# Down projection with W_down as the moving operand and one store, and the last 64 rows of W_gate and W_up on partitions 0 to 63

## The chip, the cores and the metric

The kernel runs on one core of one Trainium2 chip. The metric is the device time of one execution in microseconds (us); lower is better. Times of several executions are given as a median. The profile describes one further execution, taken by the hardware profiler.

## The reference

One step of a decoder block for four sequences (B = 4), one new token each, all data in bf16. D is 576, F is 4608. The attention has 32 query heads and 16 key heads of 128 elements and looks at the last 4096 of 16384 cached positions.

```python
h  = x + attention(layernorm(x))            # q = ln(x) @ wq; K and V from the caches; @ wo
g  = layernorm(h)
gate = g @ W_gate                           # [4, 576] @ [576, 4608]
up   = g @ W_up
hh   = gate * (gate > 0) * up               # ReGLU
out  = h + hh @ W_down                      # [4, 4608] @ [4608, 576]
```

## The kernel before

All five engines have a program of their own (`prog_sync`, `prog_pool`, `prog_act`, `prog_dve`, `prog_pe`), written out by hand. The class `Sched` gives every operation a name; a dependence on a name becomes a wait on the semaphore of the engine or transfer that makes it. Each engine runs its program in the order written. An operation that waits holds up all that follows on its engine.

**Transfers.** One list, `transfers`, in the order in which SyncE (SP in the profile) issues them: wq, then for each of the 64 pairs of sequence and key head one piece of K and one of V (1 MB each, 128 partitions), wo among them, then W_gate and W_up in four pieces of 128 rows each (`("wg", c)`, `("wu", c)`, 1.15 MB, one row of 9216 bytes per partition), then their last 64 rows (`("wg", 4)`, `("wu", 4)`), then W_down in five pieces (`WD`, of 3, 3, 3, 2 and 1 groups of 384 rows). K, V, wq and the four large pieces of W_gate and W_up use 14 slots of the tile `pool`, and a transfer into a slot waits until its last user is done (lines 188, 191 and 211 of the profile are these issues). W_down (line 223) takes the place of the K slots and waits for the last transposition of K, `("TR", 63)`; so do the last 64 rows (line 217).

The last 64 rows of W_gate and W_up: each row is cut into two halves of 2304 columns, and the 128 halves lie on 128 partitions, row r on partitions 2r and 2r + 1. For this the last 64 elements of the normalized vector are needed twice, once on even partitions and once on odd ones. A matmul with `dup` (`HDUP`) copies them to 128 partitions, and two DVE products with `par` (`HN40`, `HN41`) put zeros on the other half (`hn4`). One matmul with eight moving columns then gives a chunk of each half.

**Attention.** For each pair DVE transposes K into one of three buffers of the tile `kT` (line 344), TensorE forms scores (`qk`), and six pairs later the sum over V (`pv`). The softmax runs on batches of four pairs through DVE, POOL (the maximum over partitions, line 263) and ACT (exp, line 293). After the last pair come the projection with wo and the second layernorm, whose result is `hnT` (five chunks of D on partitions, four columns).

**Gate and up.** The weights are the stationary operand: 128 rows of D by 128 columns of F are loaded, and the four columns of `hnT` move through them. The chunks of F land in one bank of PSUM with F on partitions (`GUB`). ACT takes the relu of the gate (line 299), DVE multiplies with up (line 423); the result `hhT` has F on partitions, 36 chunks of four columns.

**Down.** W_down is the stationary operand too. For each of the 36 chunks of F and each of the five chunks of D (four of 128 columns, one of 64) one matmul with four moving columns adds to PSUM, D on partitions; that is 180 matmuls, five pieces, each piece after its own transfer. DVE adds the residual (`F2`, line 425, `F1`, line 427), transposes 32 x 32 blocks (line 429), and four small transfers store the output, two on SP and two on ACT (`out_part`, line 234). The residual is in `R_sb[:, 0]`, fp32, D on partitions.

All matmuls of `mm` have line 436 in the profile; its weight loads are the rows PEld of the same line.

Of the kernel before, what the change touches and what calls it, by code (L numbers as in the profile page):

```python
# [20 lines left out]
F = 4608  # L21
FC = F // 128
DC = 5
NPAIR = B * KVH
# [6 lines left out]
NKS = 6  # L31
# [7 lines left out]
JJ = 3  # L39
GD = 3  # L40
NG = FC // JJ
HALF = F // 2

ENGS = ("sync", "scalar", "vector", "gpsimd", "tensor")

# [54 lines left out]
def bass_sequential_preLN__sliding_block_cached__glu_gated_reglu__decode_kernel(  # L100
# [12 lines left out]
    with ExitStack() as es:  # L113
        cnt = [0]

        def sb(name, shape, dt):
            return es.enter_context(nc.sbuf_tensor(name, shape, dt))

        pool = sb("pool", [128, NSLOT, SLOT], BF16)
        wo_sb = sb("wo_sb", [128, NWO, SLOT], BF16)  # L120
        kT = sb("kT", [128, NKT, WIN // 2], FP32)
        ident_b = sb("ident_b", [128, 128], BF16)
        ones_f = sb("ones_f", [128, 128], FP32)
        sel = sb("sel", [128, 4, 4, 32], BF16)
        eps_c = sb("eps_c", [128, 1], FP32)
# [8 lines left out]
        dup = sb("dup", [64, 128], BF16)  # L134
        par = sb("par", [128, 2], FP32)
# [15 lines left out]
        hn4 = sb("hn4", [128, 2, B], BF16)  # L151
        gate_sb = sb("gate_sb", [128, FC, B], FP32)
        hhT = sb("hhT", [128, FC, B], BF16)
        h2T = sb("h2T", [128, 32], BF16)
        out_sb = sb("out_sb", [128, 32], BF16)
# [3 lines left out]
        WOB, STB, GUB, DNB, DN4 = 5, 4, 6, 7, 2  # L159
        tpv = pb[TPB][:, :].bitcast(BF16)  # L160

        S = Sched()
# [4 lines left out]
        transfers = []  # L167
# [42 lines left out]
                add((kind, c), "V", None,  # L210
                    lambda e, s, c=c, W=W: e.dma_start(out=pool[:, s, 0:F], in_=W[c * 128:(c + 1) * 128, :]))  # L211

        S4 = NKS - 1
        last_tr = [("TR", i) for i in range(NPAIR - NKS, NPAIR)]
        for u, (kind, W) in enumerate((("wg", B_W_gate), ("wu", B_W_up))):
            transfers.append(((kind, 4), f"gu4_{u}", ("TR", NPAIR - 1),
                              lambda e, u=u, W=W: e.dma_start(out=pool[:, S4, u * HALF:(u + 1) * HALF],  # L217
                                                              in_=W[512:576, :].rearrange("r (u n) -> (r u) n", u=2))))
# [8 lines left out]
        def land(name):  # L227
            return ("L",) + (name if isinstance(name, tuple) else (name,))


        def out_part(S, eng, q):
            nc_ = DC if q < 2 else DC - 1
            dst = out.rearrange("b s d -> (b s) d")
            S.dma(eng, lambda e: e.dma_start(
                out=bass.AP(tensor=dst.tensor, offset=dst.offset + 32 * q, ap=[[128, nc_], [D, B], [1, 32]]),
                in_=out_sb[32 * q:32 * q + 4 * nc_, :]), f"out{q}", deps=["OUT"], name=("STORED", q))


        def prog_sync(S):
            for name, key, free, make in transfers:  # L240
                S.dma("sync", make, key, deps=[free], name=land(name))
            for q in (0, 2):
                out_part(S, "sync", q)
            for q in (0, 2):
                S.wait("sync", ("STORED", q))


        def prog_pool(S):
            g = "gpsimd"
            S.op(g, lambda e: e.memset(eps_c[:, :], EPS), name="EPS")  # L250
            S.op(g, lambda e: e.memset(ident_b[:, :], 0.0), name="P0")
            S.op(g, lambda e: e.affine_select(out=ident_b[:, :], in_=ident_b[:, :], pattern=[[-1, 128]],  # L252
                                              compare_op=ALU.not_equal, fill=1.0, base=0, channel_multiplier=1),
                 deps=["P0"], name="IDB")
# [3 lines left out]
            S.op(g, lambda e: e.memset(h2T[:, :], 0.0), name="H20")  # L258
            for n in range(NBATCH):
                deps = [("RMAX", n)]  # L260
                if n >= 2:
                    deps.append(("SUB", n - 2))
                S.op(g, lambda e, n=n: e.partition_all_reduce(bcm[:, n % 2, :], pmax[:, n % 2, :], 128, bass_isa.ReduceOp.max),  # L263
                     deps=deps, name=("PAR", n))


        def prog_act(S):
# [31 lines left out]
            S.op(a, lambda e: e.activation(out=gate_sb[:, :, :], in_=pb[GUB][:, 0:FC * B].rearrange("p (f b) -> p f b", b=B),  # L299
                                           func=ACT.Relu),  # L300
                 deps=[("GU", 4)], name="A_GATE")
            for q in (1, 3):
                out_part(S, a, q)
            for q in (1, 3):
                S.wait(a, ("STORED", q))


        def prog_dve(S):
# [108 lines left out]
            nmr_bc = bass.AP(tensor=st2, offset=32, ap=[[40, 128], [0, DC], [1, B]])  # L417
            S.op(v, lambda e: e.tensor_tensor(out=tmp5[:, :, :], in0=R_sb[:, 0, :, :], in1=rstd_bc, op=ALU.mult), deps=["S7"], name="N1")
            S.op(v, lambda e: e.tensor_tensor(out=hnT[:, :, :], in0=tmp5[:, :, :], in1=nmr_bc, op=ALU.add), deps=["N1"], name="N2")
            for u in range(2):  # L420
                S.op(v, lambda e, u=u: e.tensor_scalar(out=hn4[:, u, :], in0=pb[STB][:, 256:256 + B], scalar1=par[:, u:u + 1], scalar2=None, op0=ALU.mult),
                     deps=["HDUP"], name=f"HN4{u}")
            S.op(v, lambda e: e.tensor_tensor(out=hhT[:, :, :], in0=pb[GUB][:, FC * B:2 * FC * B].rearrange("p (f b) -> p f b", b=B),  # L423
                                              in1=gate_sb[:, :, :], op=ALU.mult), deps=["A_GATE"], name="D_HHT")
            S.op(v, lambda e: e.tensor_tensor(out=h2T[0:64, 16:20], in0=pb[DN4][0:64, 0:B], in1=R_sb[0:64, 0, 4, :], op=ALU.add),  # L425
                 deps=["DOWN4", "H20"], name="F2")
            S.op(v, lambda e: e.tensor_tensor(out=h2T[:, 0:16], in0=pb[DNB][:, 0:16],
                                              in1=R_sb[:, 0, 0:4, :].rearrange("p c b -> p (c b)"), op=ALU.add), deps=["DOWN"], name="F1")
            S.op(v, lambda e: e.transpose(out=out_sb[:, :], in_=h2T[:, :]), deps=["F1", "F2"], name="OUT")


        def prog_pe(S):
            t = "tensor"

            def mm(o, l, r, start, stop, deps=(), name=None, skip=False):
                S.op(t, lambda e: e.matmul(o, lhsT=l, rhs=r, start=start, stop=stop, skip_group_check=skip),  # L436
                     deps=deps, name=name, signal=name is not None)
# [83 lines left out]
                           name="ATTN" if n == DC - 1 and k == H - 1 else None)  # L521
                        first = False
            mm(pb[STB][:, 128:168], ones_f[:, :], R_sb[:, :, :, :], True, True, deps=["D_R"], name="STAT")
            mm(pb[STB][:, 256:256 + B], dup[:, :], hnT[0:64, 4, :], True, True, deps=["N2"], name="HDUP")
            first = True
            gub = pb[GUB][:, 0:2 * FC * B].rearrange("p (u x) -> p u x", u=2)

            def cols(ap, fc):
                g, j = divmod(fc, JJ)
                x0 = g * 128 * JJ + j  # L530
                return ap[:, x0:x0 + 127 * JJ + 1:JJ]
# [6 lines left out]
                           deps=[land((kind, c))] + (["N2"] if first else []) if f == 0 else [], skip=True)  # L538
                        first = False
            for u, kind in ((0, "wg"), (1, "wu")):  # L540
                o = gub[:, u, :].rearrange("p (v x) -> p v x", v=2)
                for f in range(FC // 2):
                    last = u == 1 and f == FC // 2 - 1
                    mm(o[:, :, f * B:(f + 1) * B], cols(pool[:, S4, u * HALF:(u + 1) * HALF], f), hn4[:, :, :], False, last,
                       deps=[land((kind, 4)), "HN41"] if f == 0 else [], name=("GU", 4) if last else None, skip=True)
            first = True
            for k, (g0, g1) in enumerate(WD):
                deps = [land(("wd", k))] + (["D_HHT"] if first else [])
                for n in (4, 0, 1, 2, 3):
                    w = 128 if n < 4 else 64  # L550
                    for g in range(g0, g1):
                        wv = wd_sb[:, g, :].rearrange("p (j n) -> p j n", n=D)
                        for j in range(JJ):
                            last = k == len(WD) - 1 and g == g1 - 1 and j == JJ - 1
                            name = {4: "DOWN4", 3: "DOWN"}.get(n) if last else None
                            o = pb[DNB][:, n * B:(n + 1) * B] if n < 4 else pb[DN4][0:64, 0:B]
                            mm(o, wv[:, j, n * 128:n * 128 + w], hhT[:, g * JJ + j, :], g + j == 0 and n in (0, 4),
                               last and n >= 3, deps=deps, name=name, skip=True)
                            deps = []
# [37 lines left out]
```

## Time and profile before

| what | value |
|---|---|
| median of three runs | 395.9 us (395.9 to 397.0) |
| the profiled execution's own time | 396.46 us |
| its span, first to last instruction | 393.9 us |
| TensorE matmuls, weight loads, busy share | 4946, 4946, 38% and 36% |
| VectorE (DVE), ScalarE (ACT), POOL, busy share | 45%, 19%, 2% |
| read from HBM | 159.58 MB, 405 GB/s over the span |
| W_down's issues on SP, five | 353.8 to 373.9 us, 1.4 to 7.6 us each |
| W_down's first and last matmul group | from 379.74, from 388.09 us |
| the stores' issue | from 390.45 us |

The profiled execution's time holds 2.6 us around its span (launch and end). Times in the profile count from the span's start. In the timeline a row gives start, length, engine, line, operation, result and operands, count, and in brackets the idle time before it with what ended it. In a table by stage a row gives the stage, TensorE's busy time and number of instructions, its granted clock, the mean busy share of the core's 16 DMA engines and what they moved in GB/s. The trace also holds each DMA packet with its start, length and size, and the time of each semaphore increment of a transfer.

### The profile page before, as it was taken

The page shows a single profiled execution, that of the slowest core. Times are in us where ns is not written, and L with a number is a line of the kernel's source. Part 1 is how long each engine was busy: PE and PEld are TensorE (multiplying, and loading weights), DVE is VectorE, ACT ScalarE, POOL GpSimd, SP SyncE. Part 2 cuts the span into 40 slices and gives each one's busy share as a digit, 9 for nine tenths or more (in the row PEclk, how much of TensorE's full clock was granted, in tenths as well). Part 3 has the DMA queues.
Part 4 walks back from the last instruction along what each step waited for, and adds up shares of the span by engine and source line. Part 5 has one row for each costly group of instructions (what it writes and reads, how often), then busy time and mean ns, then how long its engine had stood idle before and what let it go on. Part 6 is the DMA issues. An engine that isn't in the chain of part 4 may idle for free.

```text
span 393.9 us, 10596 instructions
## 1 busy us (share of the span) xinstructions
PE 150.5 (38%) x4946; PEld 143.0 (36%) x4946; DVE 175.6 (45%) x160; ACT 75.3 (19%) x270; POOL 8.6 (2%) x27
## 2 busy tenths in 40 slices
PE   0253532113334333333243333333433333456644
PEld 0253432113334333333233333333433333446643
DVE  0578542245435555555455545453545455302000
ACT  4024030400404040404040404040212121400000
POOL 0200000000000000000000000000000000000000
DMA  8999999999999999999999999999999999999982
GB/s 313 424 418 421 418 414 421 418 416 423 419 417 420 421 418 418 422 419 418 420 422 418 418 420 421 417 421 423 418 419 421 421 419 418 421 423 420 411 361 83
DMA packets 23436, 160.25 MB, mean 407 GB/s; under 512 B 2526, under 2 KB 2530, under 8 KB 5474
## 3 DMA queue, kind: packets, MB, share of 16 engines
q1 hardware_dynamic: 23341, 159.59, 97.8%
q8 instruction: 38, 0.62, 0.6%
q10 hardware_dynamic: 53, 0.01, 0.0%
q14 instruction: 4, 0.03, 0.0%
HBM read 159.58 MB, written 0.00 MB: 405 GB/s over the span
## 4 chain that ended last, share of the span: by engine, by line
DMA 76%; DVE 8%; SPq 7%; PE 4%; issue 3%; ACT 0%; POOL 0%; POOLq 0%
DMA pool<-in_A_k_cache_dram 66%; DVE kT L344 7%; DMA pool<-in_A_v_cache_dram 6%; DMA pool<-in_B_W_down_dram 5%; SPq L223 4%; PE pb L436 4%; SPq L191 1%; SPq L188 1%; DVE sel L318 1%; SPq L205 1%; DVE qblk L382 0%; ACT xn_bf L276 0%; SPq L217 0%; PE pb L443 0%; SPq L211 0%
## 5 line engine op out<-in xcount | busy, mean ns | idle before, releaser
L344 DVE STREAM_TRANSPOSE kT<-pool 128x2048 f32<-128x2048 f32 x64 | 147.5, 2309 | 134.1 <-DMA pool<-in_A_k_cache_dram 134.0
L436 PE MATMUL pb<-qblk,kT 128*128 128x8 bf16 x2048 | 64.9, 169 | 200.6 <-DVE kT L344 197.8
L436 PEld LDWEIGHTS pb<-qblk,kT 128*128 128x128 bf16 x2048 | 59.6, 104 | 206.2 <-DVE kT L344 203.0
L293 ACT ACTIVATE prob<-s_sb 32x64 bf16<-32x64 f32 x256 | 65.9, 257 | 251.3 <-DVE s_sb L360 248.5
L436 PE MATMUL pb<-prob,pool 128*128 128x2 bf16 x2048 | 63.2, 165 | 7.1 <-DMA pool<-in_A_v_cache_dram 4.0
L436 PEld LDWEIGHTS pb<-prob,pool 128*128 128x128 bf16 x2048 | 59.4, 104 | 7.4 <-DMA pool<-in_A_v_cache_dram 4.2
L350 DVE TENSOR_REDUCE pmax<-pb 128x8 f32<-128x256 f32 x16 | 6.8, 424 | 17.8 <-PE pb L436 17.8
L263 POOL PARTITION_ALL_REDUCE bcm<-pmax x16 | 5.9, 367 | 318.6 <-DVE pmax L350 318.6
L436 PE MATMUL pb<-hnT,pool 128*128 128x4 bf16 x288 | 8.3, 166 | 3.1 <-DMA pool<-in_B_W_gate_dram 1.6
L436 PEld LDWEIGHTS pb<-hnT,pool 128*128 128x128 bf16 x288 | 8.0, 104 | 3.4 <-DMA pool<-in_B_W_gate_dram 1.7
L436 PE MATMUL pb<-hhT,pool 128*128 128x4 bf16 (+1 forms) x180 | 7.0, 173 | 5.7 <-DMA pool<-in_B_W_down_dram 5.7
L436 PEld LDWEIGHTS pb<-hhT,pool 128*128 128x128 bf16 (+1 forms) x180 | 6.5, 114 | 6.2 <-DMA pool<-in_B_W_down_dram 6.1
L367 DVE TENSOR_REDUCE rowsum<-prob 128x8 f32<-128x256 bf16 x16 | 6.1, 382 | 4.3 <-ACT prob L293 4.3
L443 PE MATMUL pb<-ident_b,xn_bf 4*128 4x4 bf16 (+1 forms) x5 | 0.4, 174 | 16.7 <-ACT xn_bf L276 16.7
L423 DVE TENSOR_TENSOR hhT<-pb,gate_sb 128x144 bf16<-128x144 f32 x1 | 0.3, 306 | 13.8 <-ACT gate_sb L299 13.8
L360 DVE TENSOR_TENSOR s_sb<-pb,bcm 128x256 f32<-128x256 f32 x16 | 6.2, 387 | 0.5 <-POOL bcm L263 0.5
L443 PEld LDWEIGHTS pb<-ident_b,xn_bf 4*128 4x128 bf16 (+1 forms) x5 | 0.3, 105 | 16.7 <-ACT xn_bf L276 16.7
L436 PE MATMUL pb<-oX,wo_sb 128*128 128x4 bf16 (+1 forms) x160 | 5.5, 172 | 1.3 <-issue 0.9
L436 PEld LDWEIGHTS pb<-oX,wo_sb 128*128 128x128 bf16 (+1 forms) x160 | 5.3, 114 | 1.5 <-issue 0.9
L318 DVE COPY sel<-ident_b 128x128 bf16<-128x128 bf16 x4 | 2.4, 1127 | 7.7 <-POOL ident_b L252 7.7
L425 DVE TENSOR_TENSOR h2T<-pb,R_sb 64x4 bf16<-64x4 f32 x1 | 0.2, 153 | 11.7 <-PE pb L436 11.7
L436 PE MATMUL pb<-xnT,pool 128*128 128x4 bf16 x128 | 3.6, 166 | 0.0
(76 smaller groups left out, 37.6 us busy)
## 6 DMA issues: line engine op xcount, KB each, us to landing
pool<-in_A_k_cache_dram SPq DMA_DIRECT2D x64, 1024.0 KB, 26.9
pool<-in_A_v_cache_dram SPq DMA_DIRECT2D x64, 1024.0 KB, 27.2
wo_sb<-in_A_wo_dram SPq DMA_DIRECT2D x4, 1152.0 KB, 24.7
pool<-in_B_W_gate_dram SPq DMA_DIRECT2D x4, 1152.0 KB, 20.0
pool<-in_B_W_up_dram SPq DMA_DIRECT2D x4, 1152.0 KB, 21.4
pool<-in_A_wq_dram SPq DMA_DIRECT2D x4, 1024.0 KB, 8.5
pool<-in_B_W_down_dram SPq DMA_DIRECT2D x3, 1296.0 KB, 25.9
pool<-in_B_W_down_dram SPq DMA_DIRECT2D x1, 864.0 KB, 17.8
```

Source lines behind the costliest of these rows:

```text
L188: add(("K", i), "K", ("TR", i), lambda e, s: e.dma_start(out=pool[:, s, 0:WIN], in_=kv(A_k_cache, i)))
L191: add(("V", i), "V", ("PV", i), lambda e, s: e.dma_start(out=pool[:, s, 0:WIN], in_=kv(A_v_cache, i)))
L205: lambda e, s, g=g: e.dma_start(out=wo_sb[:, g, :].rearrange("p (q x) -> p q x", q=2), in_=A_wo[g * 1024:(g + 1) * 1024, :].rearrange("(q ...
L223: lambda e, g0=g0, g1=g1: e.dma_start(out=wd_sb[:, g0:g1, :], in_=B_W_down[g0 * 128 * JJ:g1 * 128 * JJ, :].rearrange("(g p j) n -> p g (j ...
L263: S.op(g, lambda e, n=n: e.partition_all_reduce(bcm[:, n % 2, :], pmax[:, n % 2, :], 128, bass_isa.ReduceOp.max), deps=deps, name=("PAR", n))
L293: S.op(a, lambda e, n=n, t4=t4, g=g, sv=sv: e.activation(out=prob[32 * g:32 * g + 32, n % 3, :, 8 * t4:8 * t4 + 8, :], in_=sv[32 * t4:32 * ...
L318: S.op(v, lambda e, ce=ce: e.tensor_copy(out=sel[:, ce, :, :], in_=bass.AP(tensor=ident_b, offset=64 * (ce // 2) + ce % 2, ap=[[128, 128], ...
L344: S.op(v, lambda e: e.transpose(out=dst, in_=src), deps=deps, name=("TR", i))
L350: S.op(v, lambda e: e.tensor_reduce(out=pmax[:, n % 2, :], in_=pb[SC0 + n % 2][:, 0:NB * T * 2].rearrange("p (r t h) -> p r h t", r=NB, h= ...
L360: S.op(v, lambda e: e.tensor_tensor(out=s_sb[:, n % 2, :].rearrange("p (r t h) -> p r t h", r=NB, h=2), in0=pb[SC0 + n % 2][:, 0:NB * T * ...
L367: S.op(v, lambda e: e.tensor_reduce(out=rowsum[:, b, 8 * q:8 * q + 8], in_=prob[:, n % 3, :, :, :].rearrange("p r t h -> p r h t"), axis=A ...
L436: S.op(t, lambda e: e.matmul(o, lhsT=l, rhs=r, start=start, stop=stop, skip_group_check=skip), deps=deps, name=name, signal=name is not None)
```

## The change

Three things are changed, all behind the attention.

1. The last 64 rows of W_gate and W_up go, uncut, to partitions 0 to 63 of the tile `kT`, which the transpositions of K no longer need then. Sixteen transfers of eight rows do this: each takes every fourth partition of a block of 32. They wait for the last scores, `("QK", 63)`. `hn4`, `HDUP` and the two products go; 72 matmuls over 64 rows with four moving columns take the place of 36 over 128 rows with eight.
2. In the down projection `hhT` is the stationary operand (four columns), and W_down moves: two matmuls of 288 columns for each chunk of F, into two banks of PSUM, with the four sequences on partitions 0 to 3. The residual comes into the same sums by six fp32 matmuls of `R_sb` with an identity, `ident_f`, which POOL makes at the start.
3. ACT copies the first 288 columns to `out_sb`, DVE the other 288, and SP stores them with one transfer of four rows.

```diff
-        S4 = NKS - 1
-        last_tr = [("TR", i) for i in range(NPAIR - NKS, NPAIR)]
+        gu4 = kT[:, :, :].rearrange("p n x -> p (n x)").bitcast(BF16)
         for u, (kind, W) in enumerate((("wg", B_W_gate), ("wu", B_W_up))):
-            transfers.append(((kind, 4), f"gu4_{u}", ("TR", NPAIR - 1),
-                              lambda e, u=u, W=W: e.dma_start(out=pool[:, S4, u * HALF:(u + 1) * HALF],
-                                                              in_=W[512:576, :].rearrange("r (u n) -> (r u) n", u=2))))
+            for i in range(8):
+                p0 = 32 * (i // 4) + i % 4
+                transfers.append(((kind, 4) if i == 7 else None, f"gu4_{u}", ("QK", NPAIR - 1),
+                                  lambda e, p0=p0, u=u, W=W: e.dma_start(out=gu4[p0:p0 + 29:4, u * F:(u + 1) * F],
+                                                                         in_=W[512 + p0:512 + p0 + 29:4, :])))
...
-            for q in (0, 2):
-                out_part(S, "sync", q)
-            for q in (0, 2):
-                S.wait("sync", ("STORED", q))
+            S.dma("sync", lambda e: e.dma_start(out=out.rearrange("b s d -> (b s) d"), in_=out_sb[:, :]), "outdma",
+                  deps=["OUT0", "OUT1"], name="STORED")
+            S.wait("sync", "STORED")
...
+            S.op(g, lambda e: e.memset(ident_f[:, :], 0.0), name="P1")
+            S.op(g, lambda e: e.affine_select(out=ident_f[:, :], in_=ident_f[:, :], pattern=[[-1, 128]],
+                                              compare_op=ALU.not_equal, fill=1.0, base=0, channel_multiplier=1),
+                 deps=["P1"], name="IDF")
...
-            for q in (1, 3):
-                out_part(S, a, q)
-            for q in (1, 3):
-                S.wait(a, ("STORED", q))
+            S.op(a, lambda e: e.copy(out=out_sb[:, 0:HD], in_=pb[DNB][0:B, 0:HD]), deps=["DOWN0"], name="OUT0")
...
-            for u in range(2):
-                S.op(v, lambda e, u=u: e.tensor_scalar(out=hn4[:, u, :], in0=pb[STB][:, 256:256 + B], ...),
-                     deps=["HDUP"], name=f"HN4{u}")
...
-            S.op(v, lambda e: e.tensor_tensor(out=h2T[0:64, 16:20], ...), deps=["DOWN4", "H20"], name="F2")
-            S.op(v, lambda e: e.tensor_tensor(out=h2T[:, 0:16], ...), deps=["DOWN"], name="F1")
-            S.op(v, lambda e: e.transpose(out=out_sb[:, :], in_=h2T[:, :]), deps=["F1", "F2"], name="OUT")
+            S.op(v, lambda e: e.tensor_copy(out=out_sb[:, HD:D], in_=pb[DNB + 1][0:B, 0:HD]), deps=["DOWN1"], name="OUT1")
...
-            mm(pb[STB][:, 256:256 + B], dup[:, :], hnT[0:64, 4, :], True, True, deps=["N2"], name="HDUP")
...
-                for f in range(FC // 2):
-                    mm(o[:, :, f * B:(f + 1) * B], cols(pool[:, S4, u * HALF:(u + 1) * HALF], f), hn4[:, :, :], ...)
+                for f in range(FC):
+                    mm(gub[:, u, f * B:(f + 1) * B], cols(gu4[0:64, u * F:(u + 1) * F], f), hnT[0:64, 4, :], ...)
+            for u in range(2):
+                for c in range(DC):
+                    lo, hi = max(c * 128, u * HD), min(c * 128 + 128, D, (u + 1) * HD)
+                    if lo < hi:
+                        w = 128 if c < 4 else 64
+                        mm(pb[DNB + u][0:B, lo - u * HD:hi - u * HD], R_sb[0:w, 0, c, :],
+                           ident_f[0:w, lo - c * 128:hi - c * 128], c * 128 <= u * HD, False, ...)
             for k, (g0, g1) in enumerate(WD):
-                for n in (4, 0, 1, 2, 3):
-                    for g in range(g0, g1):
-                        for j in range(JJ):
-                            mm(o, wv[:, j, n * 128:n * 128 + w], hhT[:, g * JJ + j, :], ...)
+                for f in range(g0 * JJ, g1 * JJ):
+                    g, j = divmod(f, JJ)
+                    for u in range(2):
+                        mm(pb[DNB + u][0:B, 0:HD], hhT[:, f, :],
+                           wd_sb[:, g, j * D + u * HD:j * D + (u + 1) * HD], False, last, ...)
```

More of the change, by code (lines that the diff above doesn't have):

```diff
@@ L42 @@
 HALF = F // 2
+HD = D // 2
 ENGS = ("sync", "scalar", "vector", "gpsimd", "tensor")
@@ L122, in bass_sequential_preLN__sliding_block_cached__glu_gated_reglu__decode_kernel @@
         ident_b = sb("ident_b", [128, 128], BF16)
+        ident_f = sb("ident_f", [128, 128], FP32)
         ones_f = sb("ones_f", [128, 128], FP32)
@@ L150, in bass_sequential_preLN__sliding_block_cached__glu_gated_reglu__decode_kernel @@
         hnT = sb("hnT", [128, DC, B], BF16)
-        hn4 = sb("hn4", [128, 2, B], BF16)
         gate_sb = sb("gate_sb", [128, FC, B], FP32)
         hhT = sb("hhT", [128, FC, B], BF16)
-        h2T = sb("h2T", [128, 32], BF16)
-        out_sb = sb("out_sb", [128, 32], BF16)
+        out_sb = sb("out_sb", [B, D], BF16)
         pb = [es.enter_context(nc.psum_tensor(f"pb{i}", [128, 512], FP32)) for i in range(8)]
         SC0, OB0, SUMB, QB, QR, TPB = 0, 2, 4, 5, 6, 7
-        WOB, STB, GUB, DNB, DN4 = 5, 4, 6, 7, 2
+        WOB, STB, GUB, DNB = 5, 4, 6, 2
         tpv = pb[TPB][:, :].bitcast(BF16)
@@ L228, in land @@
             return ("L",) + (name if isinstance(name, tuple) else (name,))
[L231 to L236, printed above, removed]
         def prog_sync(S):
             for name, key, free, make in transfers:
-                S.dma("sync", make, key, deps=[free], name=land(name))
-            for q in (0, 2):
-                out_part(S, "sync", q)
-            for q in (0, 2):
-                S.wait("sync", ("STORED", q))
+                S.dma("sync", make, key, deps=[free], name=land(name) if name else None)
+            S.dma("sync", lambda e: e.dma_start(out=out.rearrange("b s d -> (b s) d"), in_=out_sb[:, :]), "outdma",
+                  deps=["OUT0", "OUT1"], name="STORED")
+            S.wait("sync", "STORED")
         def prog_pool(S):
@@ L257, in prog_pool @@
             S.op(g, lambda e: e.memset(R_sb[:, :, :, :], 0.0), name="R0")
-            S.op(g, lambda e: e.memset(h2T[:, :], 0.0), name="H20")
+            S.op(g, lambda e: e.memset(ident_f[:, :], 0.0), name="P1")
+            S.op(g, lambda e: e.affine_select(out=ident_f[:, :], in_=ident_f[:, :], pattern=[[-1, 128]],
+                                              compare_op=ALU.not_equal, fill=1.0, base=0, channel_multiplier=1),
+                 deps=["P1"], name="IDF")
             for n in range(NBATCH):
@@ L419, in prog_dve @@
             S.op(v, lambda e: e.tensor_tensor(out=hnT[:, :, :], in0=tmp5[:, :, :], in1=nmr_bc, op=ALU.add), deps=["N1"], name="N2")
-            for u in range(2):
-                S.op(v, lambda e, u=u: e.tensor_scalar(out=hn4[:, u, :], in0=pb[STB][:, 256:256 + B], scalar1=par[:, u:u + 1], scalar2=None, op0=ALU.mult),
-                     deps=["HDUP"], name=f"HN4{u}")
             S.op(v, lambda e: e.tensor_tensor(out=hhT[:, :, :], in0=pb[GUB][:, FC * B:2 * FC * B].rearrange("p (f b) -> p f b", b=B),
                                               in1=gate_sb[:, :, :], op=ALU.mult), deps=["A_GATE"], name="D_HHT")
[L425 to L429, printed above, removed]
+            S.op(v, lambda e: e.tensor_copy(out=out_sb[:, HD:D], in_=pb[DNB + 1][0:B, 0:HD]), deps=["DOWN1"], name="OUT1")
         def prog_pe(S):
@@ L540, in prog_pe @@
             for u, kind in ((0, "wg"), (1, "wu")):
-                o = gub[:, u, :].rearrange("p (v x) -> p v x", v=2)
-                for f in range(FC // 2):
[L543 to L546, printed above, removed]
-            for k, (g0, g1) in enumerate(WD):
-                deps = [land(("wd", k))] + (["D_HHT"] if first else [])
-                for n in (4, 0, 1, 2, 3):
-                    w = 128 if n < 4 else 64
-                    for g in range(g0, g1):
-                        wv = wd_sb[:, g, :].rearrange("p (j n) -> p j n", n=D)
-                        for j in range(JJ):
[L554 to L559, printed above, removed]
@@ new lines, in prog_pe @@
+                for f in range(FC):
+                    last = u == 1 and f == FC - 1
+                    mm(gub[:, u, f * B:(f + 1) * B], cols(gu4[0:64, u * F:(u + 1) * F], f), hnT[0:64, 4, :], False, last,
+                       deps=[land((kind, 4))] if f == 0 else [], name=("GU", 4) if last else None, skip=True)
+            for u in range(2):
[3 more added lines that the diff above has]
+                        w = 128 if c < 4 else 64
+                        mm(pb[DNB + u][0:B, lo - u * HD:hi - u * HD], R_sb[0:w, 0, c, :], ident_f[0:w, lo - c * 128:hi - c * 128],
+                           c * 128 <= u * HD, False, deps=["D_R", "IDF"] if u == 0 and c == 0 else [], skip=True)
@@ new lines, in prog_pe @@
+            for k, (g0, g1) in enumerate(WD):
+                deps = [land(("wd", k))] + (["D_HHT"] if k == 0 else [])
+                for f in range(g0 * JJ, g1 * JJ):
+                    g, j = divmod(f, JJ)
+                    for u in range(2):
+                        last = f == FC - 1
+                        mm(pb[DNB + u][0:B, 0:HD], hhT[:, f, :], wd_sb[:, g, j * D + u * HD:j * D + (u + 1) * HD], False, last,
+                           deps=deps, name=f"DOWN{u}" if last else None, skip=True)
+                        deps = []
```

## The prediction

> **What bounds the kernel now.** I read the chain of waits first. Its shares by line are:
>
> ```profile
> DMA pool<-in_A_k_cache_dram 66%; DVE kT L344 7%; DMA pool<-in_A_v_cache_dram 6%; DMA pool<-in_B_W_down_dram 5%; SPq L223 4%; PE pb L436 4%; SPq L191 1%; SPq L188 1%; DVE sel L318 1%; SPq L205 1%; DVE qblk L382 0%; ACT xn_bf L276 0%; SPq L217 0%; PE pb L443 0%; SPq L211 0%
> ```
>
> Nearly all of the span is transfers, and the page's slices show 411 to 424 GB/s from the second to the third last. The change touches nothing before 352.8 us, so the question is the last 41 us. The timeline of the end (start, length, what; idle before it) shows their order:
>
> ```profile
> 373.74 1.12 PE L436 MATMUL pb<-hnT,pool 128*128 128x4 bf16 x36 [1.49 <-DMA pool<-in_B_W_up_dram]
> 375.17 0.64 PE L436 MATMUL pb<-hn,pool 128*128 128x8 bf16 x18 [0.31 <-DMA pool<-in_B_W_gate_dram]
> 376.62 0.65 PE L436 MATMUL pb<-hn,pool 128*128 128x8 bf16 x18 [0.81 <-DMA pool<-in_B_W_up_dram]
> 377.30 0.29 ACT L299 ACTIVATE gate_sb<-pb 128x144 f32<-128x144 f32 x1 [14.91 <-PE pb L436]
> 379.74 1.70 PE L436 MATMUL pb<-hhT,pool 128*64 128x4 bf16 x45 [2.48 <-DMA pool<-in_B_W_down_dram]
> 388.09 1.88 PE L436 MATMUL pb<-hhT,pool 128*64 128x4 bf16 x45 [0.41 <-DMA pool<-in_B_W_down_dram]
> 390.21 0.21 DVE L429 STREAM_TRANSPOSE out_sb<-h2T 128x32 bf16<-128x32 bf16 x1
> 390.45 1.65 SPq L234 DMA_DIRECT2D out_dram<-out_sb  x2
> ```
>
> TensorE waits for each piece of W_down and is done (389.97) 0.9 us after the last has landed (389.1). But the transfers themselves are uneven. Table by stage (TensorE busy, clock, share of the 16 DMA engines that are busy, GB/s):
>
> ```profile
> 380.00:381.00 1.00, 1.00 (x33) 1.00 0.98 397
> 381.00:382.00 1.00, 0.44 (x17) 1.00 0.72 294
> 383.00:384.00 1.00, 1.00 (x30) 1.00 0.53 218
> 385.00:386.00 1.00, 0.01 (x1) 1.00 0.54 218
> 387.00:388.00 1.00, 0.68 (x26) 1.00 0.37 138
> ```
>
> From 383 to 387 half of the engines are busy. The semaphore increments that the trace records for the last W_down piece agree: eight come at 380.9 to 383.0 us, eight at 387.2 to 389.1. The reason is in the page:
>
> ```profile
> q8 instruction: 38, 0.62, 0.6%
> ```
>
> These 16 KB packets (1.0 to 1.1 us each) fetch instructions. Followed packet by packet they fall in turn on the same eight engines, and each puts its engine back by about 1.4 us; the gap between the two halves grows through the whole span. I call the halves early and late. Every full transfer ends with the late ones.
>
> **Moving rows 512 to 575 of gate and up.** Before: two transfers of 128 pieces of 4608 bytes, eight on every engine each; 16 packets of 0.18 us (their records) = 2.9 us on each engine. After: 16 transfers of eight rows of 9216 bytes. How many engines carry eight rows? A transfer over 128 partitions shows 16 increments; that of x, with four rows, shows 5; those of the output, with five and four blocks, show 6 and 5, one of them written at once. So one engine for each row or block, and eight here. Which eight? Of x's four engines one (its packet took 1.09 us, so it can be told) is an early one when its packets are followed, a second very likely is, two can't be told from others. I take it that the eight are the early engines. Then late engines save 2.9 us of work, and early ones get 16 packets of about 0.35 us instead of 2.9 us, so 2.8 more. Last W_down piece: late 389.1 - 2.9 = 386.2, early 383.0 + 2.8 = 385.8. The other pieces land late at 379.7, 382.8, 385.9 and 388.0 now, so at 376.9, 380.0, 383.1 and 385.2.
>
> [...]
>
> SP issues 16 instead of 2. At 0.43 us each (L217) and 0.05 between, 7.7 instead of 1.0 us, so the first W_down issue, behind them in SP's queue, goes from 353.8 to 360.5. Price nothing: the late engines then hold work until about 373.7 (W_up's piece 3), and SP today stands 7.3 and 7.6 us in two of the W_down issues for want of room. At over about 1.3 us an issue this cover would be gone. They wait for the last QK, at 328, and kT is free then.
>
> **Gate and up on TensorE.** HDUP, the two HN4 products and their wait go: they lie beside the 216 matmuls from 363.4 on, so nothing. The rows come as 72 matmuls of 64 rows instead of 36. The early engines deliver them by about 373.2 (367.5 for W_up's piece 3, plus 5.6), so nothing waits: W_up's piece 3 still starts at 373.74, 108 matmuls follow at 26.7 ns (the spacing of the 4-column streams) = 2.9, start of the last 376.6, its end 376.8. Now it is 377.27: 0.5 us earlier. ACT and DVE take 0.66 as now: hhT at 377.45.
>
> **The residual by identity matmuls.** Six fp32 matmuls on 576 moving columns, run as two passes each like the STAT matmul, before the wait for hhT. Price by rows: STAT with 40 columns against the row sums with 32, 415 against 401 ns, so 1.75 ns a column and pass, 576 x 2 x 1.75 = 2.0 us. Lower bound 0.3 (0.5 ns a column), upper 2.8 (12 x 0.235, STAT's spacing). Their ident_f is made by POOL in the first stage, behind what others wait for there; POOL's reduces then stand idle 318.6 us in all for DVE, so it costs nothing. From 376.65 they end at 378.65 (377.0 to 379.5), behind hhT and the first piece (376.9): W_down's start.
>
> **W_down moving.** 180 matmuls go (6.8 us, but beside the transfers); 72 with 288 moving columns come. Their weights have 4 columns; 64 columns load in 53.6 ns (the 128*64 rows' spacing), hidden behind 288 columns. No row has 288. The rows by form:
>
> ```profile
> L436 PE MATMUL pb<-qblk,kT 128*128 128x8 bf16 x2048 | 64.9, 169 | 200.6 <-DVE kT L344 197.8 <-ACT qblk L280 2.9
> L436 PE MATMUL pb<-prob,pool 128*128 128x2 bf16 x2048 | 63.2, 165 | 7.1 <-DMA pool<-in_A_v_cache_dram 4.0 <-ACT prob L293 3.1
> L436 PE MATMUL pb<-hn,pool 128*128 128x8 bf16 x36 | 1.3, 169 | 1.1 <-DMA pool<-in_B_W_up_dram 0.8 <-DMA pool<-in_B_W_gate_dram 0.3
> L436 PE MATMUL pb<-qT_sb,sel 128*128 128x128 bf16 x4 | 0.6, 307 | 0.4 <-DVE qT_sb L380 0.4
> ```
>
> Upper end: the four 128-column matmuls at 22.2 us start 106 ns apart once they queue, 0.83 ns a column: 240 ns, 72 x 0.24 = 17.3 us. Lower end: from 2 to 8 columns a steady matmul grows from 165 to 168 ns (169 with first ones of bursts), 0.5 ns a column: 144 ns, 10.4 us. I take the lower: it rests on thousands of matmuls up to 377 us, the other on four in TensorE's first 6 us of work. The first W_down matmuls may still cost more, later ones less.
>
> [...]
>
> Start 378.65 + 71 x 0.144 = 388.9 for the last start. Each piece is there before its turn (380.0 against 381.2, 383.1 against 383.8, 385.2 against 386.4, 386.2 against 388.1): TensorE no longer waits, and it is the bound. Its last matmul ends 0.3 later (166 ns and 284 columns more): 389.2.
>
> **The end.** F2, F1 and the transpose go, two copies of 4x288 come, one on ACT beside the other on DVE. DVE's casts from PSUM take 0.29 for 128 and 0.68 for 512 columns: 0.45 for 288, ACT no more (0.29 for 144). Out ready at 389.7 with two handovers. One issue instead of two in a row on each of two queues: the first of today is issued at 390.45 and lands at 392.6, the second at 393.4. So 2.15 us instead of 3.0: landing 391.85, and 0.45 to the end as now: span 392.3.
>
> 392.3 against 393.9 is 1.6 us less. The profiled execution took 396.5 us with its launch, the median of the three runs is 395.9; on it I forecast 394.3.
>
> **The rivals.**
> 1. Wide matmuls stay at 0.83 ns a column. For it: the only wide row. Against it: the growth of thousands of small ones, though their ends are modelled. 6.9 us more: 401.2, slower. It decides from about 165 ns a matmul: there the gain is gone.
> 2. The eight-row transfers run on late engines. Then the first piece lands at 379.7 + 2.8 = 382.5, and W_down starts 3.9 us later than forecast: 398.2, slower. For it: two of x's engines can't be told, and one late engine among the eight is enough. Against it: the early one that can.
> 3. The share doesn't shift (the rows spread over all engines after all). First piece at 379.7, start 1.1 later: 395.4, no change. Against it: x's five increments.
> 4. A matmul under 114 ns. Then W_down follows the transfers: 386.2 + 6 x 0.114 and the same end, 390.2, so 392.2. For it: the first two wide matmuls start 80 ns apart, which may leave a column under 0.5 ns.
>
> **How the numbers follow.** Forecast (115 to 165 ns a matmul) 0.46, with its own range 392.3 to 395.8; rivals 0.20, 0.15, 0.08 and 0.11. About 0.3%, 1.2 us, is what a measurement can tell from no change. Of the forecast's 0.46, 0.37 lies under 394.7; with rival 4 faster is 0.48. The other 0.09 and rival 3 make 0.17 for the same. Rivals 1 and 2 make 0.35 slower. Range 392.1 to 398.2 holds all but rival 1.
>
> **What would show it.** Right: DMA share near 1 until 385 and gone by 387; increments of the last piece within 3 us; one unbroken run of 72 matmuls from about 378.7, with no wait for W_down, 120 to 165 ns apart; landing 2.2 us after the store's issue. Wrong: increments of the last piece up to 392, TensorE waiting for the first piece beyond 380, or matmuls 240 ns apart to the end.

## The result and the profile after

The changed kernel takes 396.87 us (median of 13 runs), the kernel before 395.9: ratio 1.002, 95% interval 1.0011 to 1.0029. It is 0.2% slower, within what I called no change; I had forecast 394.3. Its profiled execution took 395.5 us (span 393.7), about 1.4 us less than its typical run, so a second profile is shown with the first experiment.

The chain of waits, shares by line:

```profile
DMA pool<-in_A_k_cache_dram 66%; DVE kT L336 7%; DMA pool<-in_A_v_cache_dram 6%; DMA pool<-in_B_W_down_dram 5%; PE pb L421 5%; SPq L218 3%; SPq L191 1%; SPq L224 1%; SPq L188 1%; DVE sel L310 1%; SPq L205 1%; DVE qblk L374 0%; ACT xn_bf L271 0%; PE pb L428 0%; DVE out_sb L414 0%
```

The chain still goes through a W_down transfer; behind it there are now 4.6 us of matmuls (line 421) where there was 1.9. The timeline of the end, TensorE, SP's issues and the copies:

```profile
362.75 3.56 PE L421 MATMUL pb<-hnT,pool 128*128 128x4 bf16 x123 [2.26 <-DVE hnT L411]
363.12 13.97 SPq L224 DMA_DIRECT2D pool<-in_B_W_down_dram  x5
369.19 3.70 PE L421 MATMUL pb<-hnT,pool 128*128 128x4 bf16 x128 [2.88 <-issue]
375.12 1.17 PE L421 MATMUL pb<-hnT,pool 128*128 128x4 bf16 x37 [2.23 <-issue]
376.21 2.34 PE L421 MATMUL pb<-hnT,kT 64*128 64x4 bf16 x72
378.48 2.17 PE L421 MATMUL pb<-ident_f,R_sb 128*4 128x128 f32 x12
380.58 5.68 PE L421 MATMUL pb<-pool,hhT 128*4 128x288 bf16 x36
386.84 4.57 PE L421 MATMUL pb<-pool,hhT 128*4 128x288 bf16 x36 [0.57 <-DMA pool<-in_B_W_down_dram]
391.45 0.45 DVE L414 CAST out_sb<-pb 4x288 bf16<-4x288 f32 x1 [12.23 <-PE pb L421]
391.99 0.31 SPq L235 DMA_DIRECT2D out_dram<-out_sb  x1
```

Gate and up run in three blocks with idle gaps of 2.88 and 2.23 us that end with "issue", that is, with nothing the profile names; W_down starts at 380.58 instead of the forecast 378.65, and its 72 matmuls are not one run: they wait for the third piece. The table by stage (matmuls in brackets, then granted clock, DMA share, GB/s):

```profile
381.00:382.00 1.00, 1.00 (x6) 1.00 0.90 370
383.00:384.00 1.00, 1.00 (x10) 1.00 0.86 349
385.00:386.00 1.00, 1.00 (x11) 1.00 0.28 114
387.00:388.00 1.00, 1.00 (x10) 1.00 0.13 52
389.00:390.00 1.00, 1.00 (x10) 1.00 0.05 21
```

The half of the engines that before were busy until 387 is gone, as forecast. In its place stands 0.13 up to 389: two engines of 16, alone. The increments of the last W_down piece say the same: two at 380.0 and 380.2, twelve from 383.8 to 386.1, two at 389.9. The eight-row transfers show who the two are: W_up's eight bring 64 increments with their data, eight a transfer; 48 come from 368.8 to 373.1 and 16 from 374.9 to 377.3, two at a time. So six of the eight engines that carry the rows are early ones and two are late ones. Matmuls go from 6 to 10 or 11 in a microsecond while the clock column stays at 1.00.

The instruction packets are as many as before:

```profile
q8 instruction: 38, 0.62, 0.6%
```

### The profile page after: what moved, and what is told of

Same layout as the page of the kernel before. It is cut to its first block, busy times and chain, and to the rows that moved or that the text cites. A ratio compares the mean times of both kernels' runs of the same rounds, so it can differ in the third digit from the quotient of the medians.

```text
span 393.7 us, 10482 instructions
## 1 busy us (share of the span) xinstructions
PE 156.8 (40%) x4885; PEld 145.0 (37%) x4885; DVE 175.3 (45%) x156; ACT 75.6 (19%) x271; POOL 9.0 (2%) x28
## 4 chain that ended last, share of the span: by engine, by line
DMA 77%; DVE 9%; SPq 6%; PE 5%; issue 3%; ACT 0%; POOL 0%; POOLq 0%
DMA pool<-in_A_k_cache_dram 66%; DVE kT L336 7%; DMA pool<-in_A_v_cache_dram 6%; DMA pool<-in_B_W_down_dram 5%; PE pb L421 5%; SPq L218 3%; SPq L191 1%; SPq L224 1%; SPq L188 1%; DVE sel L310 1%; SPq L205 1%; DVE qblk L374 0%; ACT xn_bf L271 0%; PE pb L428 0%; DVE out_sb L414 0%
## 5 line engine op out<-in xcount | busy, mean ns | idle before, releaser
L421 PE MATMUL pb<-pool,hhT 128*4 128x288 bf16 x72 | 10.3, 306 | 0.6 <-DMA pool<-in_B_W_down_dram 0.6
L421 PEld LDWEIGHTS pb<-pool,hhT 128*4 128x4 bf16 x72 | 6.3, 90 | 4.4 <-DMA pool<-in_B_W_down_dram 1.1
```

## The experiments

Each is an edit of the changed kernel unless it says otherwise. Ratio is against the kernel before, run beside it. "Start" is W_down's first matmul and "last piece" the landing of its last piece; span, start and last piece are from the profiled execution, in us. The kernels named "no eight-row" leave out the last 64 rows of gate and up, so they show times and not a usable kernel.

| kernel | median us | ratio (95%) | span | start | last piece |
| --- | --- | --- | --- | --- | --- |
| before | 395.9 | | 393.9 | 379.7 | 389.1 |
| changed | 396.87 | 1.0011 to 1.0029 | 393.7 | 380.6 | 389.9 |
| changed, again | 397.15 | 1.0018 to 1.0039 | 395.0 | 382.0 | 391.3 |
| W_down half alone | 394.62 | 0.9951 to 0.9976 | 392.5 | 379.4 | 388.8 |
| eight-row half alone | 398.22 | 1.0042 to 1.0066 | 396.4 | 382.2 | 391.6 |
| residual early | 397.28 | 1.0020 to 1.0037 | 395.6 | 382.3 | 391.7 |
| six rows, 10 apart | 407.47 | 1.0267 to 1.0297 | 406.0 | 392.9 | 402.0 |
| four and eight rows | 402.9 | one run | 401.1 | 388.0 | 397.3 |
| sixteen rows | 401.30 | 1.0116 to 1.0142 | 399.7 | 386.8 | 395.9 |
| W_down half, residual early | 394.94 | 0.9953 to 0.9978 | 393.5 | 379.6 | 389.1 |
| eight rows, 8 apart | 406.38 | 1.0236 to 1.0276 | 405.4 | 392.5 | 401.6 |
| no eight-row transfers | 394.82 | 0.9956 to 0.9979 | 393.5 | 380.7 | 386.0 |
| half dose | 395.66 | 0.9975 to 0.9995 | 393.8 | 380.7 | 390.0 |
| W_down half, seven pieces | 394.05 | 0.9933 to 0.9959 | 392.2 | 379.1 | 388.9 |
| no eight-row, HDUP back | 393.57 | 0.9914 to 0.9940 | 391.6 | 378.7 | 386.3 |
| changed, HDUP back | 396.94 | 1.0000 to 1.0023 | 395.2 | 382.0 | 391.4 |

**The changed kernel again** (no edit).

> The changed kernel itself, a second time with a profile. Its profiled execution (span 393.7) was 1 to 1.7 us shorter than its other runs (394.7 to 395.4), so this asks which of its stalls vary. Theory 1 (two of the eight engines that carry the eight-row transfers are late ones, and TensorE waits for its own instructions in gate and up): again two increments of the last W_down piece near 389.9 and twelve by 386.1; gate and up end at 378.5 to 380, with two idle stretches of 2 to 4 us that end with nothing the profile names; the difference of 1 to 1.7 us lies in those stretches. Rival (the wide matmuls are what varies): gate and up end at 378.5 as before, and W_down takes more than 10.8 us from its first to its last matmul.

```profile
376.70 1.16 PE L421 MATMUL pb<-hnT,kT 64*128 64x4 bf16 x36
378.77 1.16 PE L421 MATMUL pb<-hnT,kT 64*128 64x4 bf16 x36 [0.91 <-DMA kT<-in_B_W_up_dram]
379.86 2.17 PE L421 MATMUL pb<-ident_f,R_sb 128*4 128x128 f32 x12
381.96 5.46 PE L421 MATMUL pb<-pool,hhT 128*4 128x288 bf16 x36
```

This is the typical run. The two engines are there again, but their increments come 1.2 to 1.4 us later (391.1 and 391.3), and so does all that waits for them: the last of W_up's eight-row transfers, which lands at 378.7 and holds the last 36 matmuls, and W_down's first piece, 381.9. So the difference lies in these landings and not in the gaps, which are as long as before (2.61 and 2.50): the expectation had the two engines right and the place of the variation wrong. The difference is there before the rows: in both runs the late engines finish W_up's fourth piece in two groups, at 371.7 to 372.2 and 372.9 to 373.5. The two engines' first rows of W_gate land at 372.1 in the shorter run and at 373.2 and 373.5 here. One packet takes 0.35 us, so they had finished that piece at about 371.8 there, in the first group, and at about 372.9 and 373.2 here, in the second. The groups lie about 1.4 us apart, which is what one 16 KB packet costs an engine; so the two had probably one fewer behind them in the shorter run. The trace does not name the engine of a packet, so this last step is argued.

**Each half alone.** In the first run (the W_down half) the last 64 rows are loaded and multiplied as in the kernel before, with its two transfers, HDUP, HN4 and 36 matmuls. In the second (the eight-row half) W_down's matmuls and the four stores are those of the kernel before. The diff shows the first run's transfers:

```diff
- for i in range(8): ... gu4[p0:p0 + 29:4, u * F:(u + 1) * F]
+ pool[:, S4, u * HALF:(u + 1) * HALF], hn4 on 128 partitions
```

> Only the second half of the change: W_down moving and one store; the last 64 rows of gate and up as before. Theory 1: pieces of W_down land as before (379.7, 382.8, 385.9, 388.0, 389.1), gate and up end near 377.3, the residual matmuls at 379.5 to 380.1, first W_down matmul near 380, the first ten wide ones 240 ns apart and the others 123; the last follows its piece by some 1 us, 390.2 to 390.6, and 2.3 us later the span ends: 392.6 to 393, 1 us (0.2 to 0.3%) faster than before. Rival (TensorE is the bound in W_down, whatever the transfers do): W_down takes as long as in the changed kernel, 10.8 us, and the span is 393.3 to 393.8, no gain over the changed kernel's profiled run.

```profile
376.87 2.17 PE L424 MATMUL pb<-ident_f,R_sb 128*4 128x128 f32 x12
379.43 5.48 PE L424 MATMUL pb<-pool,hhT 128*4 128x288 bf16 x36 [0.40 <-DMA pool<-in_B_W_down_dram]
385.70 4.57 PE L424 MATMUL pb<-pool,hhT 128*4 128x288 bf16 x36 [0.78 <-DMA pool<-in_B_W_down_dram]
```

> Only the first half of the change: the last 64 rows of gate and up by eight-row transfers, 72 matmuls of 64 rows; W_down and the four stores as before. Theory 1: the last W_down piece lands at 389.9 on two engines instead of 389.1, gate and up end 1 us later than before (378.3 to 378.6), W_down's last matmul ends 0.9 us after the last piece, 390.8, and 3.9 us later the span ends: 394.7, 0.8 us (0.2%) slower than before. Rival (the eight-row transfers bring what I forecast for them and the loss is all in W_down's matmuls): last piece by 386.5, span near 391.5.

```profile
388.50 1.69 PE L433 MATMUL pb<-hhT,pool 128*64 128x4 bf16 x45 [1.45 <-DMA pool<-in_B_W_down_dram]
390.61 1.88 PE L433 MATMUL pb<-hhT,pool 128*64 128x4 bf16 x45 [0.42 <-DMA pool<-in_B_W_down_dram]
```

The W_down half gains 1.3 us, a little more than the 1 us expected; W_down follows its transfers (waits of 0.40 and 0.78 us). The eight-row half loses 2.3 us, not 0.8: its last piece lands at 391.6, 2.5 after that of the kernel before, as in the typical run above. -1.3 + 2.3 = +1.0, the whole change. So the loss is in the eight-row half and not in the wide matmuls.

**The residual ahead of gate and up** (the six matmuls moved to behind STAT).

> The changed kernel with its six residual matmuls moved ahead of gate and up, right after the sums of squares, where TensorE stands idle for the normalisation (2.2 us). Theory 1: W_down's first piece lands at 380.5 anyway, so the start moves by no more than 0.1 us; TensorE has then done nothing wide just before, so more of the first wide matmuls are 240 ns apart (about 18 instead of 10, some 1 us), but the wait for piece 2 (0.6 to 0.9 us) takes that up: span the same within 0.4 us. Rival (the residual stands in the way of W_down): start 1.3 us earlier, after hhT at 379.2, and the span 1 to 2 us shorter.

```profile
363.40 6.14 PE L421 MATMUL pb<-hnT,pool 128*128 128x4 bf16 x216 [0.15 <-DVE hnT L411]
379.18 1.16 PE L421 MATMUL pb<-hnT,kT 64*128 64x4 bf16 x36 [1.64 <-DMA kT<-in_B_W_up_dram]
382.34 11.00 PE L421 MATMUL pb<-pool,hhT 128*4 128x288 bf16 x72 [2.00 <-DMA pool<-in_B_W_down_dram]
```

No gain, as theory 1 said: TensorE stands 2.00 us before W_down with the residual long done. And 216 matmuls now run without a gap (a 16 KB instruction packet comes at 363.3, where the changed kernel got it at 366.6), so the gaps of 2 to 3 us are not the loss either while the rows land at 379.1. Sixteen matmuls 240 ns apart came before the spacing fell to 123.

**Other shapes of the same transfers**, to find which of the eight engines are late: six rows, then four for W_gate, then sixteen.

```diff
- 8 transfers: gu4[p0:p0 + 29:4], 8 rows 4 apart in a block of 32
+ 11 transfers: 6 rows 10 apart, the last 4 in a row
+ W_gate 16 transfers: 4 rows 16 apart
+ 4 transfers: 16 rows 4 apart over 64 partitions
```

> The changed kernel with the 64 rows of each matrix in eleven transfers, ten of six rows 10 apart and one of four, instead of eight of eight rows: 22 issues, 20 or 22 packets of 9216 bytes for each engine that is used. Engines that carry the rows end later by 0.35 us a packet; in the changed kernel a late engine with 16 of them ended at 391.5, so 385.9 without. Theory 1a (the two late engines are the last two of the eight): no late engine carries rows; six early ones, free at 378 to 380 without rows, get 7.7 us: last piece by 386 to 388, gate and up end by 378.5, W_down starts at 380.6 behind the residual, TensorE ends near 390.6, span 392.5 to 393.5, 0.6 to 0.9% less than the changed kernel. Theory 1b (a late one is among the first six): 385.9 + 7.7 = 393.6 for the last piece, span near 397, slower than the changed kernel by 0.5%. Rival (which engines carry the rows does not matter, SP's issues or the stalls in gate and up do): 22 issues instead of 16 put W_down's first issue 4 us later; same or slower than the changed kernel, with the last piece near 391 on two engines or on all.

> One look, to tell which of the eight are late: W_gate's 64 rows in sixteen transfers of four rows, W_up's in eight of eight rows as in the changed kernel. The first four engines get 24 packets (8.4 us), the other four 8 (2.8 us). Last W_down piece by theory 1a (late ones are the last two of eight): late with rows 388.7, late without 385.9, the first four 386.5 to 388.5; the last piece lands by 389. If both late ones are among the first four: two increments at 394.3. If one is: one at 394.3 and one at 388.7.

> The changed kernel with the 64 rows of each matrix in four transfers of sixteen rows 4 apart instead of eight of eight: each engine gets 8 packets of 9216 bytes, 2.8 us, as many bytes as before the change. Theory 1: pieces of W_down land as before the change (379.7 to 389.1), TensorE as with the second half of the change alone, save up to 1.3 us of stalls in gate and up; span 392.5 to 393.4, 0.5% less than the changed kernel. [...]

None came out as expected, and none tells which engines are late, because I had moved the rows to other partitions at the same time. In the changed kernel the packets of 9216 bytes behind 350 us take 0.347 to 0.356 us (5th to 95th percentile); in these three the slowest 5% take over 0.66, 0.73 and 0.71. For sixteen rows theory 1 had the pieces land as in the kernel before; the last piece, 395.9, is 6.8 us later. The next run changes the spacing alone.

**Eight rows, 8 apart** (`p0 = i; gu4[p0:p0 + 57:8, ...]`).

> The changed kernel with the eight rows of each transfer 8 partitions apart instead of 4 (same number of transfers, rows, issues and matmuls). In the runs with six, four and sixteen rows some packets of 9216 bytes took 0.66 to 0.73 us instead of 0.35. [...] Rival (it was the number of rows in a transfer or the number of issues): packets at 0.35 us and the span of the changed kernel, 394.5 to 395.4.

DMA share and GB/s of this kernel in two stages:

```profile
368.00:372.00 4.00, 0.00 (x0) 1.00 1.02 228
372.00:376.00 4.00, 3.68 (x128) 1.00 0.99 210
```

and of the changed kernel:

```profile
368.00:372.00 4.00, 2.81 (x102) 1.00 1.00 412
372.00:376.00 4.00, 1.77 (x64) 1.00 1.01 395
```

All engines are busy and move about half as much: 9.5 us of loss for a step of 8 instead of 4. The rival had the span of the changed kernel, 394.5 to 395.4; it is 405.4 with the same number of transfers and rows, so the spacing counts: the slowest 5% of the packets of 9216 bytes take 0.71 us or more, where 0.356 was the 95th percentile with rows 4 apart. Why the spacing counts is not shown, and it is not these packets alone. From 368 to 372 nearly every packet is slow, also W_down's of 3456 bytes, which at that time only the two early engines without these rows carry: 0.26 us (median) instead of 0.135. What couples these engines to the others stays open. A step of 8 would thus have cost far more than the two late engines, and a DMA share of 1 does not say that the engines run at full rate.

**The W_down half with the residual early** (the same six matmuls moved, on the W_down half).

> The second half of the change alone (394.6, span 392.5), with the residual matmuls right after the sums of squares. Theory 1: no gain, since W_down waits there for its first piece (379.4) 0.4 us after the residual has ended; more of the first wide matmuls are 240 ns apart (16 to 18 instead of 10), so the first 36 end near 386.1, 0.2 us after piece 2; span 392.5 to 392.9. Rival (the residual holds W_down up): span 391.5 to 392.

No gain here: 394.94 against 394.62, the intervals overlap. The start stays at 379.6 (379.4 in the W_down half), but 22 matmuls instead of 7 are 240 ns apart, until 385.2, and the 72 end 0.9 us later in the profiled execution. Over the runs here, 2 to 15 matmuls are 240 ns apart with the residual just ahead of W_down, 16 and 22 with it moved away.

**Without the eight-row transfers**, and half of them (`("wg", 4)` as before the change, `("wu", 4)` by eight transfers).

> The changed kernel without its sixteen eight-row transfers: the last 64 rows of gate and up are not loaded, and the matmuls on them use what lies in their place. Theory 1: without those rows the last W_down piece lands on the late engines at 385.9 to 386.3 (before the change 389.1 with 2.9 us of those rows), no two of them apart; TensorE is then the bound, as I had forecast: W_down starts at 378.7 to 380.6 behind the residual, 72 matmuls take 10.0 us without a wait, span 391 to 392.9, 2 to 4 us under the changed kernel. Rival (two engines of the eight are late for a reason other than these rows, or the loss lies in TensorE): last piece still near 390 on two engines, or the span above 393.5.

> Half a dose: W_gate's last 64 rows as before the change (128 pieces of 4608 bytes over all engines), W_up's by eight transfers of eight rows; the second half of the change in both. Theory 1: each late engine saves 1.44 us, the two that carry rows get 2.8: last piece at 390.4 on two (up to 391, by whose turn the instruction fetches are), 387.7 on the six others; gate and up end at 378.8; span 393.4 to 394.2, halfway between the second half alone (392.5) and the whole change (395). Rival (the loss comes from SP's sixteen issues of 0.62 us or from the 72 instead of 36 matmuls, not from the engines): with eight issues the last piece is at 389.1 and the span 392.5 to 392.9.

Without them the last piece lands at 386.0 and no two engines stand apart; TensorE has no wait in W_down:

```profile
369.33 3.55 PE L415 MATMUL pb<-hnT,pool 128*128 128x4 bf16 x128 [2.74 <-issue]
375.52 1.13 PE L415 MATMUL pb<-hnT,pool 128*128 128x4 bf16 x37 [2.64 <-issue]
376.58 2.08 PE L415 MATMUL pb<-hnT,kT 64*128 64x4 bf16 x72
378.59 2.17 PE L415 MATMUL pb<-ident_f,R_sb 128*4 128x128 f32 x12
380.69 10.57 PE L415 MATMUL pb<-pool,hhT 128*4 128x288 bf16 x72
```

The half dose gives two increments at 390.0, six at 385.8 to 387.5, and a time between the W_down half and the whole change (394.62, 395.66, 396.87): the loss follows the bytes on the two engines. The rival (SP's issues or the number of matmuls) expected 389.1 and a span of at most 392.9; they are 390.0 and 393.8. But the span without any of these rows, 393.5, is 0.6 over the expected range and just at the mark of its rival (the loss lies in TensorE): the two gaps of 2.74 and 2.64 us now count. The next run takes them away.

**One small matmul ahead of gate and up** (HDUP back at its place behind STAT; its result is not used), in the kernel without the eight-row transfers and in the changed kernel.

```diff
+ mm(pb[STB][:, 256:256 + B], dup[:, :], hnT[0:64, 4, :], True, True, deps=["N2"], name="HDUP")
```

> The kernel without the sixteen eight-row transfers (span 393.5, last 64 rows of gate and up not loaded), with the small matmul HDUP of the kernel before put back ahead of gate and up; its result is not used. Theory (the gaps come from late instruction packets, and whether these come in time depends on the instructions just ahead of gate and up): packet at 363.2 instead of 366.8, no gaps over 0.5 us that end with nothing named, gate and up end at 376.8 to 377.0 as I had forecast, W_down starts at 378.9 to 379.1 behind the residual, and 72 matmuls take 10.0 to 10.6 us: span 391.3 to 392.0, 1.5 to 2 us less. Rival (the gaps belong to the 72 instead of 36 matmuls or to the missing wait, not to the place): gaps stay, W_down starts at 380.7, span 393.5.

> The changed kernel with HDUP put back ahead of gate and up; its result is not used. Theory: no gaps in gate and up, but the last eight-row packets land on the two late engines at 377.3 to 379.1, so gate and up still end at 378.5 to 380.2, the first piece of W_down lands at 380.5 to 382.3 and the last at 389.9 to 391.7, span as the changed kernel, 394.5 to 395.6. Rival (the gaps are part of the loss): span 393 to 394.

```profile
363.28 5.92 PE L415 MATMUL pb<-hnT,pool 128*128 128x4 bf16 x216
370.76 1.12 PE L415 MATMUL pb<-hnT,pool 128*128 128x4 bf16 x36 [1.56 <-DMA pool<-in_B_W_gate_dram]
376.63 2.17 PE L415 MATMUL pb<-ident_f,R_sb 128*4 128x128 f32 x12
378.74 10.63 PE L415 MATMUL pb<-pool,hhT 128*4 128x288 bf16 x72
```

Both spans as expected. Without the transfers the gaps go, the instruction packet comes at 363.1 instead of 366.8, the span falls by 1.9 us, and the median time by 1.25 us to 393.57, a little less than the 1.5 to 2 expected. In the changed kernel the packet comes early too (363.6), the gaps go, and the time stays: 396.94.

**The W_down half in finer pieces.**

```diff
- WD = [(g, g + GD) for g in range(0, NG - GD, GD)] + [(NG - GD, NG - 1), (NG - 1, NG)]
+ WD = [(g, g + 2) for g in range(0, NG - 2, 2)] + [(NG - 2, NG - 1), (NG - 1, NG)]
```

> The second half of the change alone, with W_down in seven pieces (five of two groups, two of one) instead of five (three of three, two, one). There TensorE had waited for the third piece until 385.7 and then had 36 matmuls before it, 4.5 us, with the last piece there at 388.8 already. Theory 1: pieces land about 2.1 us apart on the late engines, 12 matmuls take 1.5 us, so TensorE follows them and ends 0.75 us after the last piece, 389.6 instead of 390.2: span 392.0, 0.1 to 0.2% under the second half alone. Rival (two more transfers cost the engines or SP as much): same or slower than 392.5.

```profile
379.05 5.25 PE L424 MATMUL pb<-pool,hhT 128*4 128x288 bf16 x36
384.75 1.63 PE L424 MATMUL pb<-pool,hhT 128*4 128x288 bf16 x12 [0.45 <-DMA pool<-in_B_W_down_dram]
386.87 3.10 PE L424 MATMUL pb<-pool,hhT 128*4 128x288 bf16 x24 [0.49 <-DMA pool<-in_B_W_down_dram]
```

394.05 us, 0.14% under the W_down half (its runs 393.97 to 394.28, those of the W_down half 394.33 to 394.71, in another session; the two intervals against the kernel before overlap a little, so this gain is likely, not certain) and 0.41 to 0.67% under the kernel before: the best version that still computes the whole. TensorE ends 1.1 us after the last piece, not 0.75.

## Why the prediction was wrong, step by step

**The eight engines (failed).** "I take it that the eight are the early engines" was the step that cost the gain. Six are, two are late (the increments of the eight-row transfers, 48 and 16 of 64). From one of x's four engines that could be told, and a second that very likely was early, I had generalised to eight. On the two late engines the rows cost 5.6 us instead of 2.9; the last piece lands at 391.3 in the typical run instead of 386.2 and the first at 381.9 instead of 376.9. Rival 2 said just that ("one late engine among the eight is enough"), with a chance of 0.15: its first piece, 382.5, is 0.6 off, its time, 398.2, 1.3 over the measured 396.87, about the 0.6 and the cheaper end (0.8, below) together. The measured time lies in the stated range only because that reached to this rival. A packet of 9216 bytes took as long in the changed kernel as before it (median 0.349 and 0.351 us behind 350 us), as I had priced it. What the move cost was decided by which eight engines they are.

**The end of gate and up (failed, hidden).** Forecast 376.8, profiled 378.55, typical 379.9. The step priced 72 matmuls at their spacing and did not ask whether their instructions would be there. After 123 and again after 128 matmuls TensorE stands; a 16 KB instruction packet starts at about the last matmul (at 366.6 to 367.2 in the first gap, where the kernel before got one at 363.2), and the matmuls go on 1.2 to 1.5 us after it has ended. That TensorE waits for these instructions is the reading that fits; the profile names no cause. With the eight-row transfers the rows land too late anyway, so this costs nothing; without them 1.25 us. The kernel without these rows and with HDUP has neither fault, and there the rest of the sum comes out: W_down starts at 378.74 (forecast 378.65), its matmuls end at 389.4 (389.2), and the time is 393.57 (394.3), lower by the cheaper end. It is no full proof of the forecast, since no engine carries the rows there.

**SP's issues (size wrong, conclusion right).** The issues took 0.62 us each, the first 0.78, not 0.43; the first W_down issue went out at 363.1, not 360.5. It stays far under the 1.3 us up to which I had seen cover (that SP stood 7.3 and 7.6 us in two issues for want of room was my reading; the rows show the lengths alone): the DMA share is 0.98 to 1.05 in every 2 us from 352 to 368, and the W_down pieces of the early engines without rows still land first (368.6). The last scores that the issues wait for end at 338.3, not at 328 as I had read, which is still well before 352.3, the first issue.

**The residual (right).** 2.17 us against 2.0 forecast.

**The wide matmuls (right in sum, wrong in kind).** Forecast 10.2 us to the start of the last; unbroken, without the transfers, 10.28. But no matmul took 144 ns: 13 or 14 are about 240 ns apart and the rest 123, so it was luck that 144 ns gave the right sum. What changes the spacing is not shown here: the granted clock reads 1.00 in both phases, and the change comes 3.0 to 6.1 us after dense wide matmuls began. The 0.83 ns a column of the first stage was the price of the slow phase, and 123 ns for 288 columns is 0.43 ns a column. Rival 1 held for 2 to 22 matmuls of 72.

**The end (better than forecast).** From the last matmul to the end of the span 3.1 us were forecast, 2.3 measured: the single store landed 1.3 us after its issue, not 2.15.

In sum, in the typical run: W_down starts 3.3 us later than forecast, takes 0.3 longer (waits against cheaper matmuls), and the end is 0.8 shorter: span 395.0 instead of 392.3.

## What to carry to other kernels

Here a transfer of eight rows ran on eight engines (eight increments with its data), and it ended with the latest of them, W_up's at 377.3 against 373.1 for its early engines: before work is moved to a subset of engines, each of the subset has to be known, since here two that were behind took the whole gain and more. An average over engines, or a DMA share, hides both the two that are late and a slowing of many (a share of 1.02 at 228 GB/s against 1.00 at 412). And a change with two halves is best run in halves at once: here one gained 1.3 us and the other lost 2.3.

## What was unexpected of the hardware

- With rows 8 apart instead of 4 the slowest 5% of the packets of 9216 bytes take 0.71 us or more instead of 0.35, and engines that do not carry these rows are slowed too; the DMA share reads 1 in both.
- Whether TensorE's next 16 KB of instructions come in time turned on a single small matmul before a long run of weight loads and matmuls: packet at 363.1 or at 366.8, gaps of 2.7 and 2.6 us or none. The six residual matmuls in that place did the same (363.3). Why the packet comes late, and which two of the eight engines are late, stays open.
- The change from 240 to 123 ns came 3.0 to 6.1 us after dense wide matmuls (residual or W_down) had begun, while the profile's granted clock read 1.00 throughout, and the records' mean length of one wide matmul, 306 ns, shows neither.
